# Turning keys and queries by way of DRAM in a gated recurrence with an ELU layer behind it

## The chip, the cores and the metric

The kernel runs on one core of one Trainium2 chip. The metric is the device time of one execution in microseconds (us); lower is better. A core has five engines with an instruction queue each: TensorE (PE in the profile, with PEld for its weight loads), VectorE (DVE), ScalarE (ACT), GpSimd (POOL) and SyncE (SP), which here only issues DMA transfers.

## The reference

```python
def _attn_ref(q, k, v, a_re, a_im):          # 4 sequences, 8 heads, 768 steps, 48 wide
    mag = np.sqrt(a_re * a_re + a_im * a_im)
    scale = np.minimum(mag, 0.999) / (mag + 1e-06)
    a_re_n, a_im_n = (a_re * scale, a_im * scale)
    for t in range(S):
        ar, ai = (a_re_n[:, :, t, :, None], a_im_n[:, :, t, :, None])
        new_re = ar * S_re - ai * S_im
        new_im = ar * S_im + ai * S_re
        kv = np.einsum('bhd,bhe->bhde', k[:, :, t], v[:, :, t])
        S_re, S_im = (new_re + kv, new_im)
        y[:, :, t] = np.einsum('bhd,bhde->bhe', q[:, :, t], S_re)

def _moe_ref(x, w_in, w_out):                # x: 3072 x 384, from y; 2048 hidden
    h = x @ w_in
    g = np.where(h > 0.0, h, np.exp(np.minimum(h, 0.0)) - 1.0)
    return g @ w_out
```

A complex gate decays a state of 48 x 48 for each head at each step; a query reads the real part. The result, eight heads side by side, goes through a layer with ELU. All is float32.

## The kernel before

**Units.** The work is cut into twelve units (u = 0 to 11), each of 128 steps (`C`) of two sequences (`NB`) with their eight heads (`H`). In a unit the recurrence becomes matrix products over chunks of 64 steps (`L`): queries and keys are multiplied by running products of the gates, cosine and sine parts stand side by side (`F` = 96 values for a head), masked products of keys and queries (the scores) multiply the values, and a state is carried from chunk to chunk. Then follows the ELU layer for the unit's 256 steps, written with fewer, smaller products from unit 3 on; its matmuls (`mult`, L1548, and `product`, L1410) are most of TensorE's work.

**Keys and queries turned.** VectorE writes the gated keys and queries into `kg` and `qg` with steps on the partitions (`gated`, L1020). The score matmuls (`small`, L1230; L1187 in unit 2 and L1082 in units 0 and 1) need the 96 values on the partitions: `keys_of` gives 64 columns of `kt` as the weights that are loaded, `queries_of` 64 columns of `qt` as the moving operand. In units 0 to 3 TensorE transposes them and ScalarE copies them to `kt` and `qt` (L1036, L1038). From unit 4 on they go another way, eight times in all:

- `flipped` (L1058): VectorE transposes blocks of 32 x 32 in place of the whole, in two instructions for each key ("k" or "q"), one for each sequence. The flipped queries lie in the memory of `kt`, the flipped keys in a buffer `cs`.
- `moved` (L1067): each block then has to go to another group of 32 partitions. For a block row `b` of three, SyncE issues a DMA for each of the three groups `a` that differ from it: nine transfers of 64 KB for each key.
- `stayed` (L1075): the three blocks on the diagonal stay in their partitions and are copied by POOL.

`kt` is laid out as head, then token; `qt` as block of 32 tokens, then head, then token in the block. So the pieces that a transfer writes are 128 bytes long in `kt` and 2 KB in `qt`.

**The order of work** is written out by hand: a list `first` for the beginning, and after it calls `put(time, function, unit, ...)` with times in slots, 16 to a unit, to which a table `SHIFT` adds corrections; all calls are sorted by that time, and each engine gets its instructions in the order of the calls. An engine works through its own queue in order. Waits between engines follow from what instructions read and write; a DMA's landing is a semaphore of its own, and an instruction that reads what several transfers have written waits for each of them. Around the flips stand the ELU sums of VectorE (L1564, L1573); SyncE's queue also holds the loads of the inputs (L607, L611), the stores of the output (L1439) and loads of weights for a test of their range (`test_fetch`, L693 and L696), each of which waits for VectorE's test of the one before (L707).

Of the kernel before, what the change touches and what calls it, by code (L numbers as in the profile page):

```python
# [10 lines left out]
FP32 = mybir.dt.float32  # L11
# [5 lines left out]
C = 128  # L17
L = 64
# [487 lines left out]
def kernel(  # L506
# [12 lines left out]
    nc = tc.nc  # L519
# [44 lines left out]
        for key, n in (("k", TAIL), ("q", 0))  # L564
    }
    BL = 32
    kt = cst.tile([C, NB * H, C], FP32, name="kt")
    qt = cst.tile([C, C // BL, NB * H, BL], FP32, name="qt")
    T = [cst.tile([C, NB, C // L, H], FP32, name=f"T{n}") for n in range(2)]
    NR = 48  # L570
# [149 lines left out]
    def new(tag, bufs=1, shape=None):  # L720
        return sb.tile(shape or [C, NB, H, D], FP32, tag=tag, bufs=bufs, name=tag)
# [307 lines left out]
    def transposed(u, key, n):  # L1029
        x = nat[u]  # L1030
        for h0 in range(0, H, 4):
            t = work([C, 4, C])
            for h in range(4):
                nc.tensor.transpose(t[0:F, h], gates[key][:, ts(n * H + h0 + h, F)], ident)
            if key == "k":
                nc.scalar.copy(out=kt[0:F, ds(n * H + h0, 4)], in_=t[0:F])  # L1036
                continue
            nc.scalar.copy(  # L1038
                out=qt[0:F].rearrange("p a h j -> p h a j")[:, ds(n * H + h0, 4)],
                in_=t[0:F].rearrange("p h (a j) -> p h a j", j=BL),  # L1040
            )

    def keys_of(n, h, c):
        return kt[0:F, n * H + h, ts(c, L)]

    def queries_of(n, h, c):
        return qt[0:F, ds(c * L // BL, L // BL), n * H + h]
# [1 line left out]
    def flipped(u, key, n):  # L1049

        x = nat[u]
        if n == 0:
            if key == "k":
                to = new("cs", 1, [C, NB * H, 2, D]).rearrange("p h i d -> p (h i d)")
            else:
                to = kt.rearrange("p h t -> p (h t)")[:, 0 : NB * H * F]
            x["flipped", key] = to.rearrange("p (b h j) -> p b h j", b=F // BL, j=BL)
        nc.vector.transpose(  # L1058
            out=x["flipped", key][:, :, ts(n, H)],
            in_=gates[key][:, ts(n, H * F)].rearrange("p (h b j) -> p b h j", b=F // BL, j=BL),  # L1060
        )

    def moved(u, key, b):

        for a in range(C // BL):
            if a != b:
                nc.sync.dma_start(out=block(key, a, b), in_=nat[u]["flipped", key][ts(a, BL), b])  # L1067

    def block(key, a, b):
        return kt[ts(b, BL), :, ts(a, BL)] if key == "k" else qt[ts(b, BL), a]  # L1070

    def stayed(u, key):

        for b in range(F // BL):
            nc.gpsimd.tensor_copy(out=block(key, b, b), in_=nat[u]["flipped", key][ts(b, BL), b])  # L1075

    def scores(u, n):
        x = nat[u]
# [463 lines left out]
    def mult(u, p):  # L1542

        x = nat[u]
        c = next(c for c in BANKS if p in BANKS[c])
        a = four(A(*(("t", 0) if p == 6 and u == PAIRED + 1 else IN_OF[p])))
        for m in range(4):
            nc.tensor.matmul(  # L1548
                x["c" + c][:, ts(m, C)], lhsT=a[:, m], rhs=x["mix"][p],
                start=(p == BANKS[c][0] and m == 0), stop=False, skip_group_check=True,  # L1550
            )
# [87 lines left out]
    def warm(n):  # L1639
# [4 lines left out]


    SLOTS = 16
    plan = []

    SHIFT = {
# [73 lines left out]
    def put(at, fn, *args):  # L1723
        at += shifted(fn, args)
        if fn is hidden:
            plan.append((at, len(plan), inner, args))
            plan.append((at, len(plan), elu, args))
        else:
            plan.append((at, len(plan), fn, args))
# [107 lines left out]
    for u in range(2, NU):  # L1837
        r = (u - 2) * SLOTS
        put(r + (8 if u == PAIRED else 1.5), load_a, u)
        put(r + (8 if u < PAIRED + 3 else 10), load_qk, u)  # L1840
        put(r + (8 if u < PAIRED + 3 else 12), load_v, u)
        if u == 2:
            decays_of(u, 16, 16, 17, 17, 18.4, 19.5, 19.6, 22.7, 19.8, 19.8)
            gates_of(u, 20.4, 21.6, 22.1, 22.4, 22.4, 22.6)
        else:
            sq = (r + 7.2, r + 9.6) if u < PAIRED + 4 else (r + 5.08, r + 6)
            noting = r + 11
            decays_of(u, *sq, r + 12.8, r + 13.2, r + 13.4, r + 13.5, r + 14.9, noting, r + 15.52, r + 16.6)
            gates_of(u, r + 15, r + 17.2, r + 17.4, r + 18.6, r + 18)
            put(r + 18.7, gated, u, None, ("q",))  # L1850
            put(r + 18.8, gated, u, None, ("k",))
            if u > PAIRED + 1:
                put(r + (19.45 if u < PAIRED + 4 else 21.1), table, "natural_log_exp_and_others", u)
                put(r + 15.5, table, "trig_and_small", u)
            if u > PAIRED + 1:
                put(r + 16.8, scaled, u, "k", None)
        if u > PAIRED:
            if u == PAIRED + 1:
                for n in range(NB):
                    put(r + 22 + 2 * n, transposed, u, "q", n)  # L1860
                    put(r + 23 + 2.3 * n, transposed, u, "k", n)
            else:
                for n in range(NB):
                    put(r + 19.2 + 0.5 * n, flipped, u, "q", n)
                    put(r + 21.4 + 0.5 * n, flipped, u, "k", n)
                for b in range(F // BL):
                    put(r + 19.75, moved, u, "q", b)
                for b in range(F // BL):
                    put(r + 22.15, moved, u, "k", b)
                put(r + 20.1, stayed, u, "q")  # L1870
                put(r + 23, stayed, u, "k")
            at = r + (31.3 if u + 1 < NU else 30.6)
            put(r + 28.2, small, u)
            for n in range(NB):
                put(r + 28.2, state_sums, u, 0, (n,))
                put(r + 28.2, masked, u, n)
            put(r + 28.2, state_products, u, 1)
            for n in range(NB):
                put(r + 28.2, state_sums, u, 1, (n,))
            put(at, valued_pe, u)  # L1880
            put(at, carried_pe, u)
            if u + 1 < NU:
                put(at, used, u + 1)
            put(at, copied, u)
            put(at, seam, u)
            put(r + 34.45, mixed, u)
            put(r + 34.75, mixed_rest, u)
        layer_of(u, r + 36, r + 44)
# [57 lines left out]
```

## Time and profile before

| what | value |
|---|---|
| median of three runs | 621.58 us (620.69 to 622.47) |
| the profiled execution | 621.27 us, its span 619.5 us |
| TensorE busy, weight loads busy | 605.0 us, 550.0 us |
| VectorE, ScalarE, POOL busy | 503.0, 415.8, 176.5 us |
| block transfers | 72 to `qt`, 72 to `kt`, 64 KB each |
| granted TensorE clock, mean | 0.997 |

The profile is of one execution. In a row of a group stand the line, the engine, the operation, what it writes and reads, shapes and count, then busy us and mean ns of one, then the idle time ahead of it and who ended that. Matmuls overlap in TensorE's pipeline, so the mean of one is longer than its share of the busy time. In a row of a timeline stand the start and the length of a run of like instructions in us. A matmul of float32 stands as two instructions, each with its own weight load. "SPq" marks SyncE's issues of DMAs.

### The profile page before, as it was taken

To read this page: it belongs to the slowest core of one execution; us is meant where nothing else is said; L and a number is where in the kernel's file an instruction comes from. 1 tells how busy PE (TensorE), PEld (TensorE's weight loads), DVE (VectorE), ACT (ScalarE), POOL (GpSimd) and SP (SyncE) were. 2 spreads that over 40 slices of the span, in tenths; PEclk is the share of its full clock that TensorE was granted. 3 is DMA by queue.
4 is the path that set the end of the run, shared out by engine and by line. 5 is a ranking of instruction groups with operands and counts; after the bars stand their busy time and mean duration, and the time that the engine had idled before them with its cause. 6 is when DMAs were issued, how large, how long until landed. Compare 5 with 4: busy or idle time off the path is not lost. (4 is left out here: it accounts for less than half of the span.)

```text
span 619.5 us, 16960 instructions
## 1 busy us (share of the span) xinstructions
PE 605.0 (98%) x6980; PEld 550.0 (89%) x6980; DVE 503.0 (81%) x781; ACT 415.8 (67%) x681; POOL 176.5 (28%) x240
## 2 busy tenths in 40 slices
PE   8799999999999999999999999999999999999996
PEld 6678887567899999999999999999999999999996
DVE  5788878667599899888898898899898888984482
ACT  5975674675787667776777876777777777661350
POOL 2000100103113534523524434534534422422000
PEclk9989999999999999999999999999999999999999
DMA  9978739630653253746556545546673647342101
GB/s 165 183 139 136 152 111 239 145 65 22 91 90 58 53 97 81 143 95 123 118 104 123 118 103 121 125 99 122 126 134 85 142 80 132 73 87 66 53 2 32
DMA packets 192179, 65.54 MB, mean 106 GB/s; under 512 B 168116, under 2 KB 181596, under 8 KB 192092
## 3 DMA queue, kind: packets, MB, share of 16 engines
q1 hardware_dynamic: 187920, 62.72, 51.6%
q0 software_dynamic: 3520, 1.20, 1.7%
q8 instruction: 57, 0.93, 0.7%
q10 hardware_dynamic: 652, 0.44, 0.3%
q14 instruction: 30, 0.25, 0.2%
HBM read 48.91 MB, written 4.80 MB: 87 GB/s over the span
## 5 line engine op out<-in xcount | busy, mean ns | idle before, releaser
L1410 PE MATMUL mlp<-w_out,g 128*128 128x192 f32 x640 | 112.1, 328 | 0.0
L1410 PEld LDWEIGHTS mlp<-w_out,g 128*128 128x128 f32 x640 | 104.3, 190 | 3.3 <-DVE ee L1424 0.6
L1132 POOL TENSOR_TENSOR S<-S,T 128x384 f32<-128x384 f32 x36 | 38.0, 1057 | 150.0 <-DVE S L1130 83.1
L1388 DVE TENSOR_TENSOR g<-g 128x512 f32<-128x512 f32 x80 | 60.7, 774 | 6.3 <-PE mlp L1410 4.7
L1301 PE MATMUL mlp<-x,w_in 128*128 128x256 f32 x288 | 64.1, 381 | 0.0
L1301 PEld LDWEIGHTS mlp<-x,w_in 128*128 128x128 f32 x288 | 54.7, 192 | 8.5 <-issue 0.6
L1569 ACT ACTIVATE ee<-g 128x512 f32<-128x512 f32 x63 | 39.6, 629 | 29.5 <-DVE g L1564 26.8
L1548 PE MATMUL mlp<-x,w_in 128*128 128x128 f32 x424 | 56.3, 276 | 0.1
L1410 PE MATMUL mlp<-w,g 128*128 128x192 f32 x320 | 54.5, 329 | 0.0
L1410 PEld LDWEIGHTS mlp<-w,g 128*128 128x128 f32 x320 | 51.8, 190 | 0.6
L1548 PEld LDWEIGHTS mlp<-x,w_in 128*128 128x128 f32 x424 | 51.7, 192 | 0.6 <-DVE g L1564 0.3
L1281 POOL DMA_DIRECT2D x<-y x62 | 30.6, 499 | 72.2 <-ACT y L1177 40.4
L1570 ACT ACTIVATE ee<-ee 128x512 f32<-128x512 f32 x72 | 45.4, 631 | 2.3
L1573 DVE SCALAR_TENSOR_TENSOR g<-ee,g 128x512 f32<-128x512 f32 x63 | 42.4, 682 | 2.3 <-ACT ee L1570 2.3
L1561 ACT COPY g<-mlp 128x512 f32<-128x512 f32 x36 | 20.9, 584 | 29.4 <-PE mlp L1548 29.4
L1564 DVE TENSOR_TENSOR g<-g,mlp 128x512 f32<-128x512 f32 x45 | 30.8, 684 | 8.9 <-PE mlp L1548 4.1
L1291 ACT ACT_TABLE_LOAD x24 | 30.8, 1283 | 2.1 <-issue 1.6
L921 ACT ACTIVATE n<-w 64x384 f32<-64x384 f32 (+1 forms) x60 | 28.1, 486 | 5.2 <-PE w L906 4.4
L1548 PE MATMUL mlp<-x,g 128*128 128x128 f32 x224 | 30.1, 277 | 0.0
L1268 ACT COPY x<-y 128x384 f32<-128x384 f32 x20 | 8.6, 482 | 30.9 <-PE y L1160 30.9
L1075 POOL COPY qt<-kt 32x512 f32<-32x512 f32 x24 | 24.4, 1017 | 16.3 <-PE mlp L1548 10.2
L1548 PE MATMUL y<-x,w_in 128*128 128x128 f32 x216 | 28.5, 275 | 0.0
(218 smaller groups left out, 1369.7 us busy)
## 6 DMA issues: line engine op xcount, KB each, us to landing
w<-in_moe_w_out_dram SPq DMA_DIRECT2D x8, 768.0 KB, 4.7
g<-in_moe_w_in_dram SPq DMA_DIRECT2D x24, 256.0 KB, 3.1
g<-in_moe_w_out_dram SPq DMA_DIRECT2D x24, 256.0 KB, 3.0
w<-in_moe_w_in_dram SPq DMA_DIRECT2D x16, 288.0 KB, 5.8
vn<-in_v_dram SPq DMA_DIRECT2D x24, 192.0 KB, 5.6
qt<-kt SPq DMA_DIRECT2D x72, 64.0 KB, 2.0
kt<-cs SPq DMA_DIRECT2D x72, 64.0 KB, 2.3
q<-in_q_dram SPq DMA_DIRECT2D x11, 384.0 KB, 4.7
```

The costliest lines, as they stand in the source:

```text
L921: nc.scalar.activation(out=flat(x[key][to, n : n + 1]), in_=t[of], func=AF.Exp, scale=sign)
L1132: eng.tensor_tensor(out=new_s, in0=new_s, in1=wide, op=ALU.mult)
L1281: eng.dma_start(out=x["x"][ds(j * HP + D, G), i], in_=x["y"][ds(j * HP + i * G, G)])
L1291: nc.scalar.preload_act_table_set(name)
L1301: nc.tensor.matmul(t[:, e], lhsT=w_in[:, i, ts(f + e, C)], rhs=x["x"][:, i], start=(i == 0), stop=(i == NI - 1),)
L1388: nc.vector.tensor_tensor(out=S_of(u, k, h), in0=a, in1=b, op=op)
L1410: nc.tensor.matmul(to, lhsT=a[:, m], rhs=b[:, m], start=(first and h == 0 and m == 0), stop=False, skip_group_check=True,)
L1548: nc.tensor.matmul(x["c" + c][:, ts(m, C)], lhsT=a[:, m], rhs=x["mix"][p], start=(p == BANKS[c][0] and m == 0), stop=False, skip_group_che ...
L1564: nc.vector.tensor_tensor(out=part(u, to), in0=part(u, a), in1=part(u, b), op=op)
L1569: nc.scalar.activation(out=e, in_=part(u, of), func=AF.Relu, scale=-1.0)
L1570: nc.scalar.activation(out=e, in_=e, func=AF.Exp, scale=-1.0)
L1573: nc.vector.scalar_tensor_tensor(out=part(u, to), in0=nat[u]["e", to], scalar=-1.0, in1=part(u, of), op0=ALU.add, op1=ALU.max,)
```

## The change

Keys and queries still are flipped by VectorE, but the blocks find their partitions by way of a DRAM buffer. `moved` now writes the flipped blocks out with four DMAs for each key (one for each group of 32 partitions, 192 KB), and a new function `landed` reads the whole back with one DMA of 768 KB, already in place. `stayed` and its POOL copies are gone. `landed` is put 1.5 slots (`LAND`) after `moved`. The keys' layout is turned: `kt` is now block of 32 tokens, then token, then head, so that all pieces are 2 KB for the writes and 8 KB for the read. Two columns of one head, which were neighbours, are now 16 words (64 bytes) apart; `keys_of`, the flip of the keys and ScalarE's copy in units 0 to 3 read or write `kt` with that step.

```diff
-    kt = cst.tile([C, NB * H, C], FP32, name="kt")
+    kt = cst.tile([C, C // BL, BL, NB * H], FP32, name="kt")
...
             if key == "k":
-                nc.scalar.copy(out=kt[0:F, ds(n * H + h0, 4)], in_=t[0:F])
+                nc.scalar.copy(
+                    out=kt[0:F].rearrange("p a j h -> p h (a j)")[:, ds(n * H + h0, 4)], in_=t[0:F]
+                )
...
     def keys_of(n, h, c):
-        return kt[0:F, n * H + h, ts(c, L)]
+        return kt[0:F].rearrange("p a j h -> p h (a j)")[:, n * H + h, ts(c, L)]
...
+        to = x["flipped", key]
+        if key == "k":
+            to = to.rearrange("p b j h -> p b h j")
         nc.vector.transpose(
-            out=x["flipped", key][:, :, ts(n, H)],
+            out=to[:, :, ts(n, H)],
...
-    def moved(u, key, b):
-
+    def moved(u, key):
+
+        x = nat[u]
+        x["moved", key] = to = dram.tile([F // BL, BL, C // BL, NB * H * BL], FP32, tag="moved", bufs=2, name="moved")
         for a in range(C // BL):
-            if a != b:
-                nc.sync.dma_start(out=block(key, a, b), in_=nat[u]["flipped", key][ts(a, BL), b])
-
-    def block(key, a, b):
-        return kt[ts(b, BL), :, ts(a, BL)] if key == "k" else qt[ts(b, BL), a]
-
-    def stayed(u, key):
-
-        for b in range(F // BL):
-            nc.gpsimd.tensor_copy(out=block(key, b, b), in_=nat[u]["flipped", key][ts(b, BL), b])
+            nc.sync.dma_start(
+                out=to[:, :, a].rearrange("b p n -> p b n"),
+                in_=x["flipped", key][ts(a, BL)].rearrange("p b x y -> p b (x y)"),
+            )
+
+    def landed(u, key):
+
+        nc.sync.dma_start(
+            out=(kt if key == "k" else qt)[0:F].rearrange("p a x y -> p (a x y)"),
+            in_=nat[u]["moved", key].rearrange("b p a n -> (b p) (a n)"),
+        )
...
-                for b in range(F // BL):
-                    put(r + 19.75, moved, u, "q", b)
-                for b in range(F // BL):
-                    put(r + 22.15, moved, u, "k", b)
-                put(r + 20.1, stayed, u, "q")
-                put(r + 23, stayed, u, "k")
+                put(r + 19.75, moved, u, "q")
+                put(r + 19.75 + LAND, landed, u, "q")
+                put(r + 22.15, moved, u, "k")
+                put(r + 22.15 + LAND, landed, u, "k")
```

The table `SHIFT` loses its entries for the old `moved` and `stayed` and gets like ones for the new `moved` and `landed`.

SyncE's queue at the turn of unit 6, before (L1067 are the block transfers, L693 the fetches for the test, L1439 the output's stores):

```order
L1439 DMA out_dram<-o 128x192 x3
L1067 DMA qt<-kt 32x512 x9
L693 DMA g<-in_moe_w_in_dram 128x512
L1067 DMA kt<-cs 32x16x32 x9
L693 DMA g<-in_moe_w_in_dram 128x512 x2
```

The same place after the change (L1075 are the writes of `moved`, L1082 the reads of `landed`; other lines are ten further down than before):

```order
L1449 DMA out_dram<-o 128x192 x3
L1075 DMA moved<-kt 32x3x512 x4
L693 DMA g<-in_moe_w_in_dram 128x512
L1082 DMA qt<-moved 96x2048
L1075 DMA moved<-cs 32x3x512 x4
L1082 DMA kt<-moved 96x2048
L693 DMA g<-in_moe_w_in_dram 128x512 x2
```

Eighteen transfers became ten. A test fetch stands between the queries' writes and their read, as in most units; in unit 10 one stands between the keys' writes and their read instead.

TensorE's queue at the scores of unit 5, before, with the semaphores that a matmul waits for (L1115 are products for the state, L1230 the scores; DMAHW are the semaphores of SyncE's DMAs):

```order
L1115 MATMUL w<-vn_73,kg 64x48 [waits DMAHW5_49]
L1115 MATMUL w<-vn_73,kg 64x48 x31
L1230 MATMUL y_2854<-qt,kt 64x64 [waits DMAHW3_49,DMAHW4_49,DMAHW2_49,DMAHW5_49,DMAHW0_49,DMAHW7_49,DVE_49,Pool_49]
L1230 MATMUL y_2854<-qt,kt 64x64 [waits DMAHW4_49,DMAHW6_49,DMAHW1_49,DMAHW7_49,DMAHW0_49,Pool_49]
L1230 MATMUL y_2854<-qt,kt 64x64 x14
L1230 MATMUL y_2855<-qt,kt 64x64 x16
```

And after:

```order
L1125 MATMUL w<-vn_73,kg 64x48 [waits DMAHW5_49]
L1125 MATMUL w<-vn_73,kg 64x48 x31
L1240 MATMUL y_2830<-qt,kt 64x64 [waits DMAHW7_49,DMAHW2_49,DVE_49]
L1240 MATMUL y_2830<-qt,kt 64x64 x15
L1240 MATMUL y_2831<-qt,kt 64x64 x16
```

The matmuls and their order are the same; the first waits for three semaphores in place of eight, the second for none in place of six. The order of VectorE and ScalarE is the same too but for the form of the key instructions; POOL's queue has lost its six copies a unit.

More of the change, by code (lines that the diff above doesn't have):

```diff
@@ L1054, in flipped @@
                 to = new("cs", 1, [C, NB * H, 2, D]).rearrange("p h i d -> p (h i d)")
+                to = to.rearrange("p (b j h) -> p b j h", b=F // BL, j=BL)
             else:
-                to = kt.rearrange("p h t -> p (h t)")[:, 0 : NB * H * F]
-            x["flipped", key] = to.rearrange("p (b h j) -> p b h j", b=F // BL, j=BL)
+                to = kt.rearrange("p a x y -> p (a x y)")[:, 0 : NB * H * F]
+                to = to.rearrange("p (b h j) -> p b h j", b=F // BL, j=BL)
+            x["flipped", key] = to
+        to = x["flipped", key]
+        if key == "k":
+            to = to.rearrange("p b j h -> p b h j")
         nc.vector.transpose(
-            out=x["flipped", key][:, :, ts(n, H)],
+            out=to[:, :, ts(n, H)],
             in_=gates[key][:, ts(n, H * F)].rearrange("p (h b j) -> p b h j", b=F // BL, j=BL),
         )
-    def moved(u, key, b):
+    def moved(u, key):
+        x = nat[u]
+        x["moved", key] = to = dram.tile([F // BL, BL, C // BL, NB * H * BL], FP32, tag="moved", bufs=2, name="moved")
         for a in range(C // BL):
-            if a != b:
-                nc.sync.dma_start(out=block(key, a, b), in_=nat[u]["flipped", key][ts(a, BL), b])
-    def block(key, a, b):
-        return kt[ts(b, BL), :, ts(a, BL)] if key == "k" else qt[ts(b, BL), a]
-    def stayed(u, key):
-        for b in range(F // BL):
-            nc.gpsimd.tensor_copy(out=block(key, b, b), in_=nat[u]["flipped", key][ts(b, BL), b])
+            nc.sync.dma_start(
[7 more added lines that the diff above has]
+        )
     def scores(u, n):
@@ L1646 @@
     SLOTS = 16
+    LAND = 1.5
     plan = []
```

6 rows, old and new, of the table SHIFT are left out of this document.

## The prediction

> **What bounds the kernel now.** I read the page's totals first, then the groups of instructions on TensorE, then the timeline of TensorE around the matmuls that read keys and queries.
>
> ```profile
> span 619.5 us, 16960 instructions
> PE 605.0 (98%) x6980; PEld 550.0 (89%) x6980; DVE 503.0 (81%) x781; ACT 415.8 (67%) x681; POOL 176.5 (28%) x240
> PE   8799999999999999999999999999999999999996
> PEclk9989999999999999999999999999999999999999
> ```
>
> TensorE is busy for 98% of the span, from the third slice of forty to the last but one, at full clock. A gain can only come from TensorE doing less or from its short waits; a loss comes from whatever slows its instructions. The key and query layout is read by these groups (instruction count, then busy us and mean ns):
>
> ```profile
> L1230 PE MATMUL y<-qt,kt 96*64 96x64 f32 x576 | 20.6, 223 | 0.6 <-issue 0.3
> L1082 PE MATMUL w<-qt,kt 96*64 96x64 f32 x128 | 4.6, 225 | 0.0
> L1187 PE MATMUL y<-qt,kt 96*64 96x64 f32 x64 | 2.1, 224 | 0.0
> L1230 PEld LDWEIGHTS y<-qt,kt 96*64 96x64 f32 x576 | 18.8, 138 | 2.0 <-issue 0.6
> L1230 PEldq EVENT_SEMAPHORE x56: 51/51/85, 227.7 to 554.6; - x56
> ```
>
> That is 768 score matmuls, 64 in each of twelve units, each with its own weight load of 64 key columns. The last row matters: 56 separate wait instructions stand in TensorE's queue at these matmuls, seven in each of the eight units that use block transfers (4 to 11). The order of the program shows why: the first key matmul waits for eight semaphores and the second for six, because nine transfers and three copies land separately. What that costs shows beside unit 3, whose keys come from ScalarE and whose matmuls wait for that one engine (start us, length us):
>
> ```profile
> 182.49 1.15 PE L1115 MATMUL w<-vn,kg 64*64 64x48 f32 x64
> 183.57 2.09 PE L1230 MATMUL y<-qt,kt 96*64 96x64 f32 x64
> 226.96 1.15 PE L1115 MATMUL w<-vn,kg 64*64 64x48 f32 x64
> 228.68 2.05 PE L1230 MATMUL y<-qt,kt 96*64 96x64 f32 x62 [0.27 <-issue]
> 275.64 1.15 PE L1115 MATMUL w<-vn,kg 64*64 64x48 f32 x64
> 276.81 2.39 PE L1230 MATMUL y<-qt,kt 96*64 96x64 f32 x64
> 321.72 1.15 PE L1115 MATMUL w<-vn,kg 64*64 64x48 f32 x64
> 322.86 2.47 PE L1230 MATMUL y<-qt,kt 96*64 96x64 f32 x64
> 554.60 2.19 PE L1230 MATMUL y<-qt,kt 96*64 96x64 f32 x64
> ```
>
> From the start of L1115 to the end of L1230, unit 3 takes 185.66 - 182.49 = 3.17 us, unit 4 takes 230.73 - 226.96 = 3.77, unit 5 3.56 and unit 6 3.61. Units 7, 8 and 9 read like unit 5. In units 10 and 11 the key group alone takes 2.19 against 2.09. So the waits cost 0.60 + 0.39 + 0.44 + 3 x 0.37 + 2 x 0.10 = 2.74 us of TensorE time over the run.
>
> **The change, part by part.**
>
> *Fewer waits at the key matmuls.* Both layouts now land with one read each. The new order has three semaphores (two DMAs and VectorE) at the first key matmul and none at the next. One wait instruction may remain; at 0.05 us (the 51 ns of the row above) per unit it leaves 0.4 us. Saving: 2.3 us; bounds 0 (if one late landing holds everything anyway) and 2.74.
>
> *The way of the keys through DRAM.* Before, in unit 5 (SyncE's queue, then the DMA issues with KB each and us to landing):
>
> ```profile
> 259.75 5.65 SPq L1067 DMA_DIRECT2D qt<-kt  x9
> 266.22 6.91 SPq L1067 DMA_DIRECT2D kt<-cs  x9
> kt<-cs SPq DMA_DIRECT2D x72, 64.0 KB, 2.3
> out_dram<-o SPq DMA_DIRECT2D x44, 96.0 KB, 1.7
> w<-in_moe_w_out_dram SPq DMA_DIRECT2D x8, 768.0 KB, 4.7
> ```
>
> Nine issues cost about 0.63 us each there. Now four writes of 192 KB are issued in some 2.5 us; the last, issued 1.9 us after the start, lands perhaps 2.2 us later (1.7 us for a store of 96 KB is the nearest row; twice the bytes, I add 0.5). Only then does SyncE pass on to the read, 768 KB, for which the row with the same size says 4.7 us. Together 1.9 + 2.2 + 4.7 = 8.8 us from the last key transposition. Before, the nine issues end 6.9 us after their start; the ninth is 0.6 us long or somewhat more and lands 2.3 us after it began, so about 8 to 8.6. The round trip is hardly slower, and the score matmuls start 276.81 - 266.22 = 10.6 us after it in unit 5: no wait. The short unit is 4:
>
> ```profile
> 219.81 6.85 SPq L1067 DMA_DIRECT2D kt<-cs  x9
> 313.95 7.44 SPq L1067 DMA_DIRECT2D kt<-cs  x9
> 503.13 0.41 DVE L707 TENSOR_REDUCE seen<-g 128x1 f32<-128x256 f32 x1
> 508.98 2.19 PE L1230 MATMUL y<-qt,kt 96*64 96x64 f32 x64
> ```
>
> There 219.81 + 8.8 = 228.6, where the first matmul now starts at 228.1: 0.6 us late, which I charge. In unit 6 SyncE comes to the keys at 313.95; even from there they land at 322.75, just before 322.86. In unit 10 a fetch of test weights stands between the writes and the read, and waits for VectorE's test to end at 503.54: the read lands near 504 + 4.7 = 508.7, just before 508.98. Price of this part: 0.6 us; bounds 0, and 9 us if the trip is 2 us longer everywhere (2.6 in unit 4, up to 2 in units 6 and 10, under 1 in the others).
>
> Behind the waiting read stand in SyncE's queue the next test fetch, which waits for VectorE anyway, and then the loads of q, k and v for a later unit. SyncE is through with each unit in ten issues instead of eighteen. I charge nothing.
>
> *POOL's copies go.* 24.4 + 17.2 us of POOL work leave an engine that is 28% busy and off the chain:
>
> ```profile
> L1075 POOL COPY qt<-kt 32x512 f32<-32x512 f32 x24 | 24.4, 1017 | 16.3 <-PE mlp L1548 10.2 <-DVE kt L1058 3.8 <-DMA out_dram<-o 1.4
> L1075 POOL COPY kt<-cs 32x512 f32<-32x512 f32 x24 | 17.2, 715 | 12.9 <-DVE cs L1058 4.2 <-DMA qt<-kt 4.1 <-issue 2.4
> ```
>
> Nothing is gained by itself.
>
> *Keys lie 16 words apart.* This is the open price, in three places: 768 weight loads read single words 64 bytes apart; 16 transpositions of keys on VectorE, and 16 copies on ScalarE in units 0 to 3, write so. No row of the trace shows such an access. Rows that bound it:
>
> ```profile
> L1548 PEld LDWEIGHTS mlp<-x,w_in 128*128 128x128 f32 x424 | 51.7, 192 | 0.6 <-DVE g L1564 0.3 <-ACT g L1561 0.2
> L1591 PEld LDWEIGHTS w<-seen,ones 128*1 128x1 f32 x2 | 0.1, 80 | 0.1
> L1034 PEld LDWEIGHTS w<-ident,kg 128*96 128x96 f32 x64 | 7.0, 126 | 3.2 <-ACT qt L1038 2.0 <-issue 0.4
> L1115 PE MATMUL mlp<-vn,kg 64*128 64x48 f32 x64 | 4.0, 274 | 0.0
> L671 DVE TENSOR_SCALAR wr<-w 128x768 uint32<-128x768 uint32 x16 | 8.9, 557 | 2.3 <-DMA w<-in_moe_w_out_dram 1.2 <-DMA w<-in_moe_w_in_dram 1.1
> L866 DVE TENSOR_SCALAR cs<-n 128x384 uint32<-128x384 uint32 x4 | 1.4, 360 | 0.1
> L1058 DVE STREAM_TRANSPOSE cs<-kg 128x768 f32<-128x768 f32 x16 | 15.5, 967 | 0.0
> L1036 ACT COPY kt<-w 96x512 f32<-96x512 f32 x16 | 8.5, 583 | 8.1 <-PE w L1034 8.1
> ```
>
> A load of 128 columns takes 192 ns and one of 64 takes 138, so a key column costs 0.84 ns. The loads for transpositions, 96 columns in 126 ns where one column takes 80, cost 0.48 ns a column: the path from memory can go nearly twice as fast as a key load asks. Also, L671 reads every second word (768 in 557 ns) at the pace (0.5 ns a word) at which L866 reads neighbours (384 in 360). So if single words halve the path's own pace to 0.97 ns, a key load takes 8 ns more, and 768 x 4 (two loads run side by side in the two column halves) is 3 us. If they halve the key load's pace, it lasts as long as one of 128 columns. The row for that is L1115 with 128 columns and few moving ones: 4.0 us for 64, 62.5 ns each, where keys take 20.6 / 576 = 35.8. Then 768 x 26.7 = 20.5 us. I take 0, as the half of the rows that speak at all show slack, and keep 20.5 as the far end.
>
> The Trainium skill speaks against this edit: Advanced Engine Details and Errata, section SBUF Cachelines, says that memory lines are 16 bytes, that two accesses must hit a line to hide its latency, and that one line for each access costs. By it the far end would be the sum. The step of L671 stays within its allowance, and no run here shows more.
>
> On VectorE the bound is an operation of twice the elements, L1020 with 1536 at 1.8 us: 0.83 us more for each key transposition. Around the transpositions VectorE has little room:
>
> ```profile
> L1020 DVE TENSOR_TENSOR kg<-k,cs 128x1536 f32<-128x1536 f32 (+1 forms) x12 | 21.6, 1797 | 3.2 <-ACT cs L994 3.2
> 257.00:267.00 10.00, 10.00 (x92) 10.00 (x91) 9.28 (x12) 6.17 (x11) 6.75 (x6) 1.00 0.40 82
> 267.00:277.00 10.00, 9.97 (x141) 9.62 (x139) 9.06 (x15) 6.51 (x11) 1.40 (x3) 1.00 0.56 111
> ```
>
> VectorE is busy 9.28 and 9.06 us of these ten-microsecond stretches: 1.66 us idle, just what two slow transpositions would eat. Late behind them are the sums and ELU halves (L1564, L1573) that free TensorE's banks. Bounds 0 and 0.4 us a unit, 3 us in all. On ScalarE, only the copies that a score group of units 0 and 1 waits for are on the path, four of them; at double their streaming they would take 0.4 us more each, 1.7 us. I take 0 for both.
>
> **Sum.** 621.27 (the profiled execution; 619.5 is its span, and the median of the runs is 0.3 higher) - 2.3 + 0.6 = **619.6 us**.
>
> **The rivals.**
>
> *Key loads at half pace* (slower than before). Place: the 64 weight loads at each score group; price 26.7 ns each; it decides as soon as a column costs more than about 0.9 ns, since matmul and load now run level in these groups (20.6 us busy against 18.8). For it: no row shows single words read at full pace. Against: the slack of L1034's loads. Time 619.6 + 20.5 = 640, with the writes also slow up to 645; with half of the path's pace only, 623.
>
> *Keys land late.* The round trip is 2 us longer than I add up, as the stores meet other transfers. For it: no store of 192 KB from 32 partitions stands in the trace, and DMA is 40 to 56% busy in the two stretches above. Against: SyncE's own queue holds nothing else between the writes and the read but one test fetch. Time 619.6 + 4 to 9 = 624 to 628.
>
> *Only the writes are slow.* VectorE and ScalarE pay, weight loads don't: 619.6 + 2 to 4.7 = 622 to 624.
>
> *The wait merely changes its name*: the one read landing holds the first key matmul as long as the many semaphores did. Time 621 to 622.
>
> **How the numbers follow.** Forecast 46%, own range 618.2 to 621.0; key loads slower 34% (28% at half pace or worse, 6% near 623); late landing 8%; slow writes 6%; renamed wait 6%. A measurement can tell 0.3%, 1.9 us: faster means under 619.7. The forecast lies on that edge; I give it 33 of its 46 as faster, since the bound of the saving is 2.74, and 13 as the same. To the same come the renamed wait, most of the slow writes and part of the loads near 623: 24% in all. Slower is the rest, 43%. For 8 times in 10 the range must reach into the half pace: 617.8 to 641; outside are its slower end and a larger gain.
>
> **What would show it.** Right: L1230's successor has 64 matmuls in about 2.1 us at 138 ns a load, its wait instructions drop from 56 to 8 or fewer, and the gap ahead of the group shrinks in units 4 to 9. Wrong: a load of keys reads 160 to 200 ns and the group takes near 4 us (half pace); the reading matmul shows a wait on the kt read (late landing); L1058's key transposition reads over 1.2 us (slow writes).

## The result and the profile after

| | before | after |
|---|---|---|
| median | 620.69 us (618.22 to 622.47, 5 runs) | 668.73 us (667.03 to 675.94, 5 runs) |
| ratio | | 1.0798, 95% interval 1.0737 to 1.0859 |
| profiled execution, its span | 621.27, 619.5 us | 675.94, 674.2 us |
| granted clock, mean | 0.997 | 0.954 |

The change costs 8%; the forecast was 619.6 us and its range ended at 641. The profiled execution is the longest of the five and has the lowest clock (the other four 0.968 to 0.973), so its parts add up to some 7 us more than the median.

The totals of the page after, TensorE's slices and its clock:

```profile
span 674.2 us, 16734 instructions
PE 641.2 (95%) x6980; PEld 584.1 (87%) x6980; DVE 508.2 (75%) x781; ACT 422.5 (63%) x681; POOL 136.8 (20%) x192
PE   7899999999999989999989989989999989999996
PEclk9769999999999989999989987998999998998998
```

Two things are new. TensorE is busy for 36 us more with the same 6980 matmuls, and from the fifteenth slice on six slices of 8 stand among its nines, with seven dips of the clock beside or close to them, ahead of the last slice. The clock also dips in the second and third slice, deeper than before; these lie ahead of the first keys that move through DRAM, and no run says why.

The groups that read keys, after (lines are ten further down; the last row is the wait instructions at the score matmuls):

```profile
L1240 PE MATMUL y<-qt,kt 96*64 96x64 f32 x576 | 35.1, 300 | 15.3 <-DMA kt<-moved 7.6 <-issue 5.8 <-DVE S L1140 1.5
L1092 PE MATMUL w<-qt,kt 96*64 96x64 f32 x128 | 8.4, 283 | 0.5 <-ACT kt L1036 0.5
L1197 PE MATMUL y<-qt,kt 96*64 96x64 f32 x64 | 3.8, 277 | 0.0
L1240 PEld LDWEIGHTS y<-qt,kt 96*64 96x64 f32 x576 | 33.8, 208 | 16.1 <-issue 8.8 <-DVE S L1140 5.4 <-DVE g L1583 1.4
L1240 PEldq EVENT_SEMAPHORE  x8: 51/423/3481, 246.9 to 605.1; - x8
```

A key load takes 208 ns instead of 138, and the three groups are busy for 35.1 + 8.4 + 3.8 = 47.3 us instead of 20.6 + 4.6 + 2.1 = 27.3: **20.0 us more**. Ahead of L1240 TensorE stands idle for 15.3 us instead of 0.6: **14.7 us more**. The profile puts half of it, 7.6 us, down to the landing of `kt`; 5.8 stand as "issue", for which it shows no releaser. Together that is 34.7 of the 54.7 us by which the span grew. Most of the rest is time in which TensorE's other matmuls are busy: 36.2 - 20.0 = 16.2 us more than before.

The writers of keys, after (VectorE's transpositions of keys and of queries, ScalarE's copies):

```profile
L1065 DVE STREAM_TRANSPOSE cs<-kg 128x768 f32<-128x768 f32 x16 | 23.9, 1495 | 0.0
L1065 DVE STREAM_TRANSPOSE kt<-qg 128x768 f32<-128x768 f32 x16 | 14.6, 947 | 0.0
L1036 ACT COPY kt<-w 96x512 f32<-96x512 f32 x16 | 15.6, 1076 | 10.6 <-PE w L1034 10.6
```

Keys take 1495 ns where queries, written as before, still take 947; ScalarE's copy went from 583 to 1076 ns.

Unit 5 after, on SyncE's queue and on TensorE (start us, length us):

```profile
286.06 0.32 SPq L1082 DMA_DIRECT2D qt<-moved  x1
286.27 1.47 DVE L1065 STREAM_TRANSPOSE cs<-kg 128x768 f32<-128x768 f32 x1
287.77 2.99 SPq L1075 DMA_DIRECT2D moved<-cs  x4
293.52 0.31 SPq L1082 DMA_DIRECT2D kt<-moved  x1
296.56 1.15 PE L1125 MATMUL w<-vn,kg 64*64 64x48 f32 x64
299.06 3.92 PE L1240 MATMUL y<-qt,kt 96*64 96x64 f32 x64 [1.35 <-DMA kt<-moved]
```

From the first write to the first score matmul 299.06 - 287.77 = 11.29 us pass; without the wait TensorE would have come at 297.71, after 9.94. The queries' read is issued 1.7 us ahead of the keys' first write, so the two trips overlap. The medians of the issues' landings, after, and the DMA share of a stretch of twelve microseconds from the keys' last flip on (last two columns: busy share, GB/s; before, then after):

```profile
moved<-cs SPq DMA_DIRECT2D x32, 192.0 KB, 4.2
kt<-moved SPq DMA_DIRECT2D x8, 768.0 KB, 5.8
```

```profile
266.00:278.00 12.00, 11.93 (x178) 11.51 (x179) 10.78 (x19) 8.11 (x15) 2.19 (x3) 1.00 0.51 100
```

```profile
287.00:299.00 12.00, 10.70 (x147) 10.35 (x145) 11.40 (x19) 8.14 (x14) 0.00 (x0) 1.00 0.81 220
```

Beside some waits the clock falls: in units 6, 7, 8, 10 and 11, within 1 us of the first score matmul, with waits of 1.4 to 3.1 us, but not in units 5 and 9, with 1.35 and 1.49 us. Unit 7 after, first TensorE's timeline, then the windows around it (the third figure from the end is the granted clock):

```profile
401.23 3.94 PE L1240 MATMUL y<-qt,kt 96*64 96x64 f32 x64 [2.19 <-DMA kt<-moved]
405.09 1.96 PE L1125 MATMUL w<-vn,kg 64*64 64x48 f32 x64
406.98 2.93 PE L1420 MATMUL mlp<-w_out,g 128*128 128x192 f32 x8
```

```profile
400.00:405.00 5.00, 3.77 (x64) 3.78 (x64) 1.12 (x2) 2.74 (x5) 0.83 (x1) 0.61 0.12 32
405.00:410.00 5.00, 5.00 (x77) 4.82 (x74) 2.88 (x6) 0.06 (x1) 0.83 (x1) 0.50 0.09 19
```

At a clock of 0.50 the group L1125 takes 1.96 us where it takes 1.15 in unit 5, and the eight matmuls of L1420 behind it 2.93 us where they take 1.57 there. The score group itself takes the same, 3.94 and 3.92. No such stretch stands behind a score group before the change. The page TensorE: Matmul & The Clock Gate of the Trainium skill (its part on the HAM clock gate) says that the clock knows two rates, full and half, and goes by how busy TensorE was in windows of about 3.4 us; the 0.50 here agrees.

### The profile page after: what moved, and what is told of

Read it like the earlier page. It is cut to its first block, busy times and chain, and to the rows that moved or that the text cites. A ratio compares the mean times of both kernels' runs of the same rounds, so it can differ in the third digit from the quotient of the medians.

```text
span 674.2 us, 16734 instructions
## 1 busy us (share of the span) xinstructions
PE 641.2 (95%) x6980; PEld 584.1 (87%) x6980; DVE 508.2 (75%) x781; ACT 422.5 (63%) x681; POOL 136.8 (20%) x192
## 4 chain that ended last, share of the span: by engine, by line
PE 75%; DVE 7%; DMA 7%; ACT 6%; issue 2%; SPq 1%; POOL 0%; DVEq 0%; ACTq 0%; POOLq 0%
PE mlp L1420 26%; PE mlp L1558 10%; PE mlp L1311 8%; PE y L1240 5%; PE y L1558 5%; DMA kt<-moved 3%; PE mlp L1336 3%; PE y L1170 3%; DMA moved<-cs 3%; PE y L1336 2%; PE w L854 2%; PE w L1125 2%; DVE g L1574 2%; PE y L1161 2%; DVE g L1583 2%
## 5 line engine op out<-in xcount | busy, mean ns | idle before, releaser
L1420 PE MATMUL mlp<-w_out,g 128*128 128x192 f32 x640 | 116.5, 336 | 0.0
L1420 PEld LDWEIGHTS mlp<-w_out,g 128*128 128x128 f32 x640 | 108.3, 196 | 3.5 <-DVE ee L1434 0.6
L1311 PEld LDWEIGHTS mlp<-x,w_in 128*128 128x128 f32 x288 | 54.9, 192 | 10.3 <-ACT ee L1320 1.4
L1420 PE MATMUL mlp<-w,g 128*128 128x192 f32 x320 | 54.5, 329 | 0.0
L1420 PEld LDWEIGHTS mlp<-w,g 128*128 128x128 f32 x320 | 51.8, 190 | 0.6
L1240 PE MATMUL y<-qt,kt 96*64 96x64 f32 x576 | 35.1, 300 | 15.3 <-DMA kt<-moved 7.6
L1240 PEld LDWEIGHTS y<-qt,kt 96*64 96x64 f32 x576 | 33.8, 208 | 16.1 <-issue 8.8
L1248 DVE TENSOR_TENSOR a<-y,mask 128x512 f32<-128x512 f32 x18 | 12.4, 689 | 28.3 <-PE y L1240 28.3
L1428 ACT COPY ee<-mlp 128x192 f32<-128x192 f32 x10 | 3.1, 315 | 46.4 <-PE mlp L1420 28.4
```

Of the source, the lines that this page charges most:

```text
L1240: nc.tensor.matmul(t[n][ts(c, L), ts(h, L)], lhsT=keys_of(n, h, c), rhs=queries_of(n, h, c), start=True, stop=True,)
L1311: nc.tensor.matmul(t[:, e], lhsT=w_in[:, i, ts(f + e, C)], rhs=x["x"][:, i], start=(i == 0), stop=(i == NI - 1),)
L1420: nc.tensor.matmul(to, lhsT=a[:, m], rhs=b[:, m], start=(first and h == 0 and m == 0), stop=False, skip_group_check=True,)
```

## The experiments

My theory after the result had two halves: keys 16 words apart slow whatever reads or writes them, and the trip lands late. The first four runs set them apart. All stand beside runs of the kernel before on the same chip.

| kernel | median us | before | ratio (95%) | key load ns | idle ahead of scores us | clock of the profiled run |
|---|---|---|---|---|---|---|
| step of 16 words alone | 647.78 | 619.34 | 1.0447 (1.0424 to 1.0469) | 208 | 0.0 | 0.994 |
| trip alone, 128-byte pieces | 666.79 | 619.34 | 1.0732 (1.0668 to 1.0796) | 193 | 22.0 | 0.949 |
| step of 4 words alone | 651.99 (one run) | 619.34 | | 216 | 0.1 | 0.985 |
| step of 2 words alone | 620.33 (one run) | 619.34 | | 138 | 0.6 | 0.996 |
| change, no receipts | 660.19 | 620.18 | 1.0658 (1.0614 to 1.0702) | 209 | 7.8 | 0.983 |
| change, warm matmuls | 668.17 | 620.18 | 1.0782 (1.0739 to 1.0825) | 209 | 1.6 | 0.988 |
| queries alone by DRAM | 621.42 | 620.18 | 1.0010 (0.9988 to 1.0033) | 138 | 0.0 | 0.996 |
| step of 2, keys in halves | 630.52 | 620.18 | 1.0154 (1.0116 to 1.0192) | 151 | 7.6 | 0.983 |
| change, no keys written | 655.22 | 619.75 | 1.0578 (1.0535 to 1.0621) | 209 | 0.8 | 0.992 |
| trip with step of 2 | 642.71 | 619.75 | 1.0375 (1.0319 to 1.0431) | 158 | 13.0 | 0.982 |
| change, keys' trip alone | 661.22 | 620.63 | 1.0683 (1.0633 to 1.0733) | 210 | 7.9 | 0.979 |

A mean load above 138 ns at a step of one or two words comes from stretches at half clock: in the kernel with 128-byte pieces and a clock of 0.949 the key loads have a median of 138 ns at full clock and of 227 in those stretches. At a step of 16 words, after the change, it is 207 ns in both.

### The step alone, at 16, 4 and 2 words

The kernel before with its block transfers; only the keys' layout changes.

```diff
-    kt = cst.tile([C, NB * H, C], FP32, name="kt")
+    kt = cst.tile([C, NB * H // SP, C, SP], FP32, name="kt")      # SP = 16, 4, 2
...
-        return kt[0:F, n * H + h, ts(c, L)]
+        return kt[0:F, (n * H + h) // SP, ts(c, L), (n * H + h) % SP]
```

> The kernel before with one edit: keys lie 16 words apart (token, then head), while the block transfers and POOL's copies stay. Theory A (most of the loss is the step): score groups cost what they cost after the change, 19 to 20 us over the run, ScalarE's copies and VectorE's transpositions of keys 1.07 us and 1.5 us each; with half-clock stretches behind, 645 to 655 us. Rival B (most of the loss is the late landing through DRAM): the score groups cost less than half of that once no landing is waited for, and the time is 625 to 636 us.

> The kernel before with keys 4 words (16 bytes) apart. If a whole line of 16 bytes is spent on each word, this costs as much as 16 words apart: weight loads of keys about 207 ns, the transposition of keys 1.5 us, ScalarE's copy 1.07 us. If the cost grows with the distance, all three lie clearly between that and the kernel before (138 ns, 0.97 us, 0.58 us).

> The kernel before with keys 2 words (8 bytes) apart. If a line of 16 bytes is what counts, two words share a line and nothing is lost: weight loads 138 ns, transposition 0.97 us, copy 0.58 us, time within 3 us of the kernel before. If any step costs, the loads read 160 to 207 ns and the time is over 630 us.

Groups of instructions at 16 words:

```profile
L1248 PE MATMUL y<-qt,kt 96*64 96x64 f32 x576 | 37.0, 279 | 0.0
L1100 PE MATMUL w<-qt,kt 96*64 96x64 f32 x128 | 8.3, 283 | 0.5 <-ACT kt L1037 0.5
L1205 PE MATMUL y<-qt,kt 96*64 96x64 f32 x64 | 3.8, 278 | 0.0
L1248 PEld LDWEIGHTS y<-qt,kt 96*64 96x64 f32 x576 | 35.6, 208 | 1.0
L1079 DVE STREAM_TRANSPOSE cs<-kg 128x768 f32<-128x768 f32 x16 | 24.1, 1506 | 0.0
```

At 4 words:

```profile
L1248 PEld LDWEIGHTS y<-qt,kt 96*64 96x64 f32 x576 | 37.2, 216 | 1.0 <-issue 0.2
L1079 DVE STREAM_TRANSPOSE cs<-kg 128x768 f32<-128x768 f32 x16 | 25.9, 1618 | 0.0
```

At 2 words:

```profile
L1248 PEld LDWEIGHTS y<-qt,kt 96*64 96x64 f32 x576 | 19.3, 138 | 2.0 <-issue 1.0
L1079 DVE STREAM_TRANSPOSE cs<-kg 128x768 f32<-128x768 f32 x16 | 15.5, 970 | 0.0
```

The step alone costs 28.4 us, without a wait for a landing and at a clock of 0.994: theory A's time, without the stretches at half clock that it expected behind the scores. The bound lies between 8 and 16 bytes: two words apart cost loads and transpositions nothing (ScalarE's copy took 633 ns instead of 583), four cost as much as sixteen, in one run each. That agrees with the Trainium skill, Advanced Engine Details and Errata, section SBUF Cachelines (lines of 16 bytes, two accesses to each line needed); the size of the price, 138 to 208 ns for a load of 64 columns and 970 to 1506 ns for a transposition, comes from these rows.

### The trip alone

The changed kernel with keys contiguous again. Tokens of one head then come in pieces of 128 bytes, and the keys' read is four DMAs. Later I ran the same with keys two words apart, so that the pieces are 256 bytes; at full clock a key load takes 138 ns in either.

```diff
-            out=(kt if key == "k" else qt)[0:F].rearrange("p a x y -> p (a x y)"),
+            out=qt[0:F].rearrange("p a x y -> p (a x y)"),
...
+        if key == "k":
+            for a in range(C // BL):       # contiguous keys; two words apart likewise, by pairs of heads
+                nc.sync.dma_start(
+                    out=kt[0:F, :, ts(a, BL)],
+                    in_=nat[u]["moved", key][:, :, a].rearrange("b p (h j) -> (b p) h j", j=BL),
+                )
+            return
```

> The changed kernel with keys contiguous again (head, then token); keys and queries still go through DRAM, but the keys' read is four DMAs of 192 KB in pieces of 128 bytes in place of one of 768 KB. No step of 16 words is left. Theory A: the weight loads are back at 138 ns, and only the wait for the landing is left, 1 to 3 us in each of eight units: 630 to 642 us. Rival B (the landing and the half clock behind it are most of the loss): 645 to 660 us.

> The changed kernel with keys 2 words apart; the keys' read is four DMAs of 192 KB in 256-byte pieces, the writes and the queries as in the change. Key loads read 138 ns and VectorE's key transposition 970 ns again. Theory A (the line and the late trip are two separate losses, some 27 and 21 us): 638 to 646 us, with waits of 1 to 3 us for kt in most units. Theory B (with fast loads TensorE only comes to the wait sooner, so most of the line's price is hidden by it, as in the kernel with 128-byte pieces at 666.8): 652 or more. Theory C (the short pieces were what made that kernel slow, and halves of the trip, at 630.5, gained little): 628 to 636.

The score group with 128-byte pieces:

```profile
L1243 PE MATMUL y<-qt,kt 96*64 96x64 f32 x576 | 30.5, 283 | 22.0 <-DMA kt<-moved 20.0 <-DVE g L1586 0.9 <-DVE g L1401 0.9
```

And with 256-byte pieces:

```profile
L1251 PE MATMUL y<-qt,kt 96*64 96x64 f32 x576 | 25.1, 247 | 13.0 <-DMA kt<-moved 12.8 <-issue 0.2
```

With short pieces the trip alone already costs 47 us by the medians and 45 by the ratio, above what either theory gave, which hid the answer (its profiled execution, 671.65 us, is the longest of four). With 256 bytes it costs 642.71 - 619.75 = 23.0 us, as theory A of that run had it. In its profiled execution the span is 22.6 us longer than before: 12.4 are idle time ahead of the scores, and in 7.8 TensorE is busy longer (612.8 us instead of 605.0), at a clock of 0.982. The two losses nearly add: 28.4 + 23.0 = 51.4, and the change costs 668.73 - 620.69 = 48.0.

### What makes the trip late

First the keys' read without its wait for the writes; then without the writes; then the keys' trip without that of the queries.

```diff
-            in_=nat[u]["moved", key].rearrange("b p a n -> (b p) (a n)"),
+            in_=... if key == "q" else k[0].rearrange("h s d -> (h s d)")[0 : F * NB * H * C].rearrange("(p x) -> p x", p=F),
```

> The changed kernel, but the keys' read fetches 768 KB of the same shape from the input k, so it need not wait until the four writes have landed; the writes stay, and nobody reads them (the scores of units 4 to 11 are then not the reference's). Theory A (the order of the trip is late: writes, their landing, then the read): the read lands some 5 us sooner, TensorE's wait of 17 us goes and with it the stretches at half clock; what is left is the price of the 16-word step, 648 to 652 us as in the kernel with the step alone (647.8). Theory B (the transfers themselves are too slow, whoever waits for whom): a wait on the kt read stays in most units and the time is over 660.

```diff
-        for a in range(C // BL):
+        for a in range(C // BL if key == "q" else 0):     # beside the edit above
```

> The kernel of the run without receipts (the keys' read fetches 768 KB from the input k; the scores of units 4 to 11 are not the reference's), and the four writes of the keys are left out too. The read stands behind nothing but the queries' read and lands well ahead of the scores. Theory A (what the run without receipts still lost against the kernel with the step alone, 12 us, is the read's place behind four writes and beside their traffic): no wait on kt, 645 to 651 us. Theory B (a read of 768 KB at this place, or the queries' trip, costs by itself with the 16-word step): a wait stays, 655 or more.

```diff
-                put(r + 19.75, moved, u, "q")
-                put(r + 19.75 + LAND, landed, u, "q")
```

> The changed kernel without the queries' trip: their four writes and their read are left out in units 4 to 11, so that these units use the queries of unit 3 and the scores there are not the reference's. Theory A (the two trips collide: in unit 5 the queries' read of 768 KB is issued 1.7 us ahead of the keys' first write and is still landing while these write): the keys' writes land in about 3 us instead of 4.2, their read in 5 or less instead of 5.8, TensorE's wait falls from 17 us to under 6, and the time to 650 to 656. Theory B (each trip is slow by itself, issue, landing and receipt): writes and read keep their times within 0.4 us, the wait stays over 11 us, 660 or more.

Score group without receipts:

```profile
L1240 PE MATMUL y<-qt,kt 96*64 96x64 f32 x576 | 35.1, 287 | 7.8 <-DMA kt<-in_k_dram 4.2 <-DVE g L1583 2.6 <-DVE g L1574 0.9
```

Without the keys' writes:

```profile
L1240 PE MATMUL y<-qt,kt 96*64 96x64 f32 x576 | 35.0, 283 | 0.8 <-DMA kt<-in_k_dram 0.8
L1240 PEldq EVENT_SEMAPHORE  x8: 51/51/51, 239.1 to 579.4; - x8
```

The keys' trip alone, with the landings of its DMAs and SyncE's queue in unit 5:

```profile
L1240 PE MATMUL y<-qt,kt 96*64 96x64 f32 x576 | 35.3, 289 | 7.9 <-DMA kt<-moved 6.9 <-DVE g L1583 1.0
```

```profile
moved<-cs SPq DMA_DIRECT2D x32, 192.0 KB, 3.0
kt<-moved SPq DMA_DIRECT2D x8, 768.0 KB, 5.6
```

```profile
282.41 2.21 SPq L1075 DMA_DIRECT2D moved<-cs  x4
287.50 0.32 SPq L1082 DMA_DIRECT2D kt<-moved  x1
```

Without receipts and with the keys alone the time comes out at theory B's edge (660.19 and 661.22), yet half of the idle time is gone in both (7.8 and 7.9 us of 15.3): neither theory holds whole. Alone, the keys' writes land in 3.0 us instead of 4.2, as theory A said, but the read still takes 5.6, and in unit 5 it is issued 5.09 us after the first write instead of 5.75. So the trip by itself is about 10.7 us long (5.09 + 5.6), more than the 9.94 that are there, and with the queries' trip beside it the idle time of the profiled executions doubles. Without receipts the read still lands late, behind four issues and beside their traffic: 4.2 us of its 7.8 are put down to it. Without the writes the wait is gone; whether their issues or their traffic held the read, the runs do not tell apart.

That last kernel's profiled execution (648.45 us) has what the step alone costs and nothing more, as theory A said, but its median of 655.22 is theory B's: its six runs fall into two groups: 648.45 and 648.82 at a clock of 0.992 and 0.989, and four from 654.3 to 657.3 at 0.972 to 0.975. The only trace is of the first kind, so where the clock fell in the others stays open.

It also shows the saved waits: over the run the group is busy for 35.0 us, where the step alone, with the same loads, has 37.0. The same group in unit 5, with the step alone (56 wait instructions, 7 a unit):

```profile
290.39 1.15 PE L1133 MATMUL w<-vn,kg 64*64 64x48 f32 x64
291.54 4.18 PE L1248 MATMUL y<-qt,kt 96*64 96x64 f32 x64
```

And without the keys' writes (8 in all):

```profile
289.86 1.15 PE L1125 MATMUL w<-vn,kg 64*64 64x48 f32 x64
290.94 3.98 PE L1240 MATMUL y<-qt,kt 96*64 96x64 f32 x64
```

From the start of the first to the end of the second, 5.33 us became 5.06: 0.27 us saved, where the prediction gave 0.39 to this unit.

### Does the half clock cost time of its own?

```diff
         state_products(u, 0)
+        for _ in range(8 if u > PAIRED + 1 else 0):
+            nc.tensor.matmul(t[0][:, 0:C], lhsT=ident, rhs=ident, start=True, stop=True)
```

> The changed kernel with eight matmuls of 128 x 128 on the identity ahead of the scores in units 4 to 11, into a place that the scores write over. They fill about 2 us in which TensorE waits for the keys. Theory A (after a wait of 2 us and the thin score group the clock is granted at half, and that costs 8 to 14 us by itself in the groups behind): the mean clock rises from 0.954 to 0.98 or more and the time falls to 657 to 663, although unit 4 and the shorter waits lose up to 5 us to the new matmuls. Theory B (the slow groups behind the scores are late for another reason, banks or VectorE): 668 to 674.

The new matmuls and the score group behind them, with TensorE's total:

```profile
PE 644.4 (97%) x7108; PEld 588.1 (89%) x7108; DVE 508.7 (77%) x781; ACT 422.4 (64%) x681; POOL 136.9 (21%) x192
L1238 PE MATMUL y<-ident 128*128 128x128 f32 x128 | 16.4, 281 | 0.0
L1242 PE MATMUL y<-qt,kt 96*64 96x64 f32 x576 | 35.2, 282 | 1.6 <-DMA kt<-moved 1.6
```

And TensorE's total with the step alone:

```profile
PE 629.7 (97%) x6980; PEld 572.6 (89%) x6980; DVE 508.5 (79%) x781; ACT 422.6 (65%) x681; POOL 176.5 (27%) x240
```

The new matmuls took 16.4 us of TensorE where 15.3 - 1.6 = 13.7 us of idle time went, and the clock rose from 0.954 to 0.988 in the profiled runs (0.968 to 0.973 and 0.979 to 0.983 in the others). The median did not move: 668.17 against 668.73, intervals 1.0739 to 1.0825 and 1.0737 to 1.0859. Theory A's 657 to 663 is refuted.

The price of the half clock, on which that theory rests, is not. In the profiled execution of the change TensorE is busy for 641.2 us; here for 644.4 - 16.4 = 628.0 without the new matmuls, 13.2 us less, though the score groups take the same. With the step alone, at a clock of 0.994, all matmuls but the scores take 629.7 - 49.1 = 580.6 us; in the change they take 641.2 - 47.3 = 593.9, 13.3 more, and matmul by matmul the difference lies in the stretches at half clock (2.4 us of it by the scores of unit 3, ahead of any trip). So the half clock does cost time beside the wait, some 13 us in that execution, and theory B's other reasons are not needed. That execution is the longest of its five and the one with the new matmuls the shortest of its four, so the price in a median execution is lower; what it is there no trace shows, and the equal medians do not bound it, since the new matmuls cost more than the idle time that they fill.

### Two versions that might have won

Queries through DRAM with keys as before, and, in the other, keys two words apart that go through DRAM in two halves.

```diff
+        if key == "q":                  # moved(u, "q", 0): four writes; landed: one read; keys by blocks
+            ...
```

```diff
+    def moved_keys(u, n):               # n: the sequence; four writes of 96 KB
+    ...
+    def landed_keys(u, n):              # four reads of 96 KB in 256-byte pieces
```

> The kernel before with the queries alone through DRAM (four writes, one read); keys by block transfers, one after the other, as before. Theory A (the trip hurts only where it is the last to land): the queries have the time that the keys' flips and transfers take, nothing waits for them, the key matmuls wait for fewer semaphores: 619 to 621 us, 0 to 1.4 under before. Theory B (trips crowd SyncE's queue or the DMA engines): the keys' transfers land later, score groups wait, 624 or more.

> Both through DRAM, but keys 2 words apart, and written and read back in two halves, one for each sequence (four writes of 96 KB and four reads of 96 KB in 256-byte pieces each). Theory A (the loss is the 16-byte line plus a trip that is 1 to 3 us too long): no load is slower than 140 ns, the first half lands about 2 us sooner, TensorE hardly waits, 619 to 626 us. Theory B (reads in short pieces are slow, as in the kernel with 128-byte pieces): the waits for kt stay, with half clock after them, 635 to 660.

Wait instructions at the scores, queries alone:

```profile
L1248 PEldq EVENT_SEMAPHORE  x48: 51/51/288, 227.5 to 555.5; - x48
```

Score group with keys in halves:

```profile
L1266 PE MATMUL y<-qt,kt 96*64 96x64 f32 x576 | 24.3, 240 | 7.6 <-DMA kt<-moved 7.5
```

The queries' trip hurts nothing, since it has time, but it takes away only one wait instruction a unit (56 to 48), and the time is level, 1.001 (0.9988 to 1.0033): the gain of up to 1.4 us that theory A allowed was not found. Halves bring the loss of the trip down from 23.0 to some 10 us (630.52 - 620.18 = 10.3; the ratio gives 9.6); that lies between the two theories, and the waits for `kt` stay (the profiled execution, 638.47 us, is the longest of six). No kernel here beats the one before.

## Why the prediction was wrong, step by step

**"Keys lie 16 words apart" failed first, as a choice between bounds.** I took 0 of 0 to 20.5 us for the loads. The groups grew by 20.0: the far end, worked out from L1115's 62.5 ns for each load with its matmul, was right to half a microsecond (with the step alone, where all the waits stay, they grew by 21.8), and the mechanism is the rival "Key loads at half pace". The slack of L1034's loads and the step of L671 both lay within what a line forgives, so they could not speak for this access. L671 steps 8 bytes and agrees with the kernel at two words; nothing in the trace stepped 16. The Trainium skill's section that spoke against the edit, SBUF Cachelines in Advanced Engine Details and Errata, was right, and a chance of a third was too low for a cost that the only statement on such an access supported.

**Its writers were mis-sized too.** VectorE's transpositions took 0.53 us more (the bound was 0.83). ScalarE's copies took 0.49 us more, not 0.4; with the step alone the loss is 28.4 us, of which the three score groups carry 37.0 + 8.3 + 3.8 - 27.3 = 21.8, so some 6 to 7 us more lie elsewhere, where the bounds for the writers were 3 and 1.7. Most of it stands in units 0 to 3: counted from each matmul's start to the next one's, the transpositions of L1034, some of which wait for ScalarE's copies, take 3.0 us longer there, and the matmuls of L1301 take 2.6. Of these 2.6, 1.0 is a wait for the DMA `x<-y` and 1.2 lie in a stretch at half clock, so that the writers' part in them is not shown.

**"The way of the keys through DRAM" failed by its terms.** Predicted: 1.9 + 2.2 + 4.7 = 8.8 us against a slack of 10.6. In unit 5 the read was issued 5.75 us after the first write, where 4.1 were added up, and TensorE had it 5.54 us after that; 11.29 in all. The write term came from a store of 96 KB with 0.5 us added for twice the bytes; it measures 3.0 us with the queries' trip left out and 4.2 with it. The read of 768 KB takes 5.6 and 5.8, not 4.7. The slack shrank as well, from 10.6 to 9.94. I had written that nothing else stands between the writes and the read in SyncE's queue; one that mattered stands ahead of them, the queries' read of 768 KB that was still landing. "Keys land late" named this rival and its 2 us, but its 4 to 9 us were too few: the wait came in every unit from 5 on and was 15.3 us long in all; the trip alone costs 23.0 us.

**The clock was taken to stay full.** The prediction read 0.997 and put no term into its sum for a clock that falls. Beside the late keys it fell to 0.50, and in the profiled execution of the change, at a mean of 0.954, that lengthened matmuls that do not read keys by some 13 us (2.4 of them ahead of any trip), the largest part of the growth that neither the key groups nor the waits explain.

**The rivals were kept apart, though they add.** Each was priced against the forecast; the result is two of them at once. 20.5 us for the loads and 9 for the trip would have made 649 together, and the range ended at 641.

**"Fewer waits at the key matmuls" was right in mechanism.** Wait instructions fell from 56 to 8, as said, and where keys are on time unit 5 gains 0.27 us of the 0.39 counted, and the groups of all units 2.0 of the 2.3. In the change the one that is left lasts up to 3481 ns.

**"POOL's copies go"** came out as said, 40 us of POOL less; no run tells it apart from the rest, and none shows a gain.

**Unit 10** went as described and worse: the test fetch stood between the writes and the read, and the read came late: TensorE stood idle for 2.7 us ahead of these scores.

```profile
542.19 2.33 SPq L1075 DMA_DIRECT2D moved<-cs  x4
547.08 0.40 SPq L696 DMA_DIRECT2D g<-in_moe_w_out_dram  x1
549.94 0.31 SPq L1082 DMA_DIRECT2D kt<-moved  x1
```

The prediction had the read landing at 508.7 of a start at 508.98, and here it is issued 7.75 us after the first write.

## What to carry to other kernels

Before a layout moves neighbours apart, ask for each engine that reads or writes it how many words it takes from each 16 bytes: here one word of each line made a load take half as long again, and two cost it nothing. Add up a trip through DRAM with the transfers that are still landing when it starts, not only those behind it in the queue, and compare it with the slack that the change itself leaves. Where TensorE waits, ask also what the clock does to the matmuls behind. Where two rivals act in different places, their prices add, and a range should hold the sum.

## What the runs showed of the hardware

- A load of 64 float32 key columns takes 138 ns at steps of 4 and 8 bytes, 216 at 16 and 208 at 64, in executions with a mean clock of 0.985 and more. In stretches at half clock its median is 227 at a step of 4 bytes, but at 64 bytes it is 207 there and at full clock. The same bound holds for writes: VectorE's transposition of 768 columns takes 967, 970, 1618 and 1506 ns, ScalarE's copy of 512 takes 583, 633, 1134 and 1079 ns. Sixteen bytes were slightly dearer than sixty-four, in one execution each.
- Four stores of 192 KB to DRAM, issued within 2 to 3 us, land in a median of 3.0 us with nothing of the queries under way and 4.2 beside their read; the read of 768 KB takes 5.6 to 5.8.
- At the end of an idle 2.2 us TensorE's clock fell to 0.50 and stayed there through the five microseconds from 405 to 410; in that execution it fell beside five waits of 1.4 to 3.1 us and not beside two of 1.35 and 1.49. Filling the idle time with matmuls raised the mean clock from 0.954 to 0.988 in the profiled executions, where all other matmuls together were busy for 13.2 us less; the median time did not change.
